# Turning ten more attention blocks of X by DMA, with fewer filling matmuls and a new order of the work

## The chip, the cores and the metric

The kernel runs on one core of one Trainium2 chip. The metric is the device time of one execution in microseconds (us). The program has one queue of instructions for each engine: PE (TensorE, matmuls; PEld is its weight load), DVE (VectorE), ACT (ScalarE), POOL (GpSimd) and SP (SyncE, which here only issues DMAs). Each queue is worked off in its own order; an instruction waits at the head of its queue until what it needs is there, and all behind it wait with it.

## The reference

A gated linear attention is followed by a two-layer network with a leaky ReLU. Shapes: q, k, v and f_logit are (4, 8, 768, 48), that is batch, heads, time, channel; w_in is 384 x 2048 and w_out 2048 x 384; the output is 3072 x 384. All tensors are float32.

```python
f = 1.0 / (1.0 + np.exp(-f_logit))
for t in range(S):
    state = f[:, :, t, :, None] * state + np.einsum('bhd,bhe->bhde', k[:, :, t], v[:, :, t])
    y[:, :, t] = np.einsum('bhd,bhde->bhe', q[:, :, t], state)
x = y.transpose(0, 2, 1, 3).reshape(B * S, H * D)
h = x @ w_in
out = np.maximum(0.01 * h, h) @ w_out
```

## The kernel before, in words

**Units.** Time is cut into 6 chunks of 128 steps, and a unit is one chunk of one batch element: 24 units. Units 0 to 3 are the first chunks of the four batch elements, 4 to 19 the middle chunks, 20 to 23 the last. A unit gives 128 rows of y, called X where it enters the network. Two units make a pair m; pair m holds units 2m and 2m + 1, and its network part works on 256 rows.

**Attention of a unit** from 4 on: three loads (load_part, L168) bring k, q and v; gate_pe (L338) sums the log gates of a group of four units on PE, decay_em and decay_a (L350, L353) make the decays on ACT; k_scale and q_scale (L356, L360) scale k and q on DVE or POOL into the tile kqh; cast_v (L144 or L146) makes bfloat16 v. turn_dma (L372) turns kqh by a transposing DMA into kqT (units 8 to 23; turn_pe, L369, does it on PE for units 4 to 7). score_pe (L394) forms the scores of both units of a pair, mask (L405) masks them on DVE, mix_pe (L412 and L415) gives y, and state_pe, state_dve and state_pool (L423, L431, L432, L437, L296) carry the state on. Units 0 to 3 have functions of their own whose names begin with q_: q_gate_pe L220, q_decay_act L224, casts q_k_cast and q_q_cast (L144 or L146), q_turn_pe L236, products q_k_mul and q_q_mul on DVE (L240), q_score_pe L254, masks q_mask on DVE (L265) and q_mask_pool on POOL (L261), q_mix_pe L271.

**X to the network.** y_out copies a unit's y from PSUM to the bfloat16 tile xn (on ACT or DVE). Then X is turned so that its 384 channels lie on partitions, in one of two ways. x_pe (L446) makes three transposes on PE into PSUM, and x_out copies them to xT on ACT or DVE. x_dma (L376) is one transposing DMA on SP's queue, from xn straight to xT:

```python
def x_dma(u):
    nc.sync.dma_start_transpose(out=x_part(u), in_=xns[u % R_XN])
```

Before the change units 0 to 17 take the first way and 18 to 23 the second.

**Network of a pair.** up (L456; up1, L467, for single units) is six matmuls of 256 columns, eight of them for a pair; up_act (L461) is the leaky ReLU on ACT into gT; down (L476) is eight matmuls of 384 columns for one half of a unit, two halves to a unit; put copies the result to SBUF and out_dma (L499) writes it out. The first halves of the up products (g of 0 to 3) use the first half of w_in, the others the second; each half is one DMA of POOL's queue (load_w_in, L180).

**Filling matmuls.** idle_pe(n, bank) (L138) issues n matmuls on a tile of zeros, whose result nobody reads. Before the change there are 41 ahead of the first gate sums and 2 + 2 + 3 among the first scores.

**Order.** The order is written out by hand: a list of some 800 calls, one line each, at the end of the kernel. Each engine's queue holds its instructions in the order of this list. SP's queue takes the loads, the turns and the outputs in one line, and each of its DMAs also waits for the one issued eight before it. Rings of tiles tie things together: 7 raw tiles each of k, q and v, 4 of kqh, kqT, xn and xT, 5 of gT, 8 of the output.

Of the kernel before, what the change touches and what calls it, by code (L numbers as in the profile page):

```python
# [16 lines left out]
def kernel(  # L17
# [485 lines left out]
    q_ln_act(0)  # L503
    q_k_cast(V, 1)
    q_exp_act(1)
    idle_pe(24, 0)
    q_ln_act(1)
    q_q_cast(G, 1)
    idle_pe(17, 1)
    q_gate_pe(0, 1, 2)  # L510
    q_gate_pe(0, 0, 3)
    load_part(2, 'v', v)
    q_gate_pe(1, 1, 4)
    q_decay_act(0, 0, emT, 1.0, 3)
    q_gate_pe(1, 0, 5)
    q_decay_act(0, 1, emT, 1.0, 2)
    load_part(1, 'v', v)
    q_turn_pe(khq, 1, 1, 6)
    q_decay_act(1, 1, emT, 1.0, 4)
    q_k_cast(A, 0)  # L520
    q_turn_pe(khq, 0, 0, 7)
    q_k_mul(1, 1, 6)
    q_k_mul(0, 0, 7)
    q_turn_pe(khq, 0, 1, 0)
    q_decay_act(1, 0, emT, 1.0, 5)
    q_turn_pe(khq, 1, 0, 1)
    load_part(0, 'v', v)
    q_q_cast(A, 0)
    q_turn_pe(qhq, 1, 0, 6)
    q_decay_act(0, 0, aT, -1.0, 3)  # L530
    load_w_in(0)
    load_w_in(1)
    q_k_mul(0, 1, 0)
    q_decay_act(1, 0, aT, -1.0, 5)
    load_part(3, 'v', v)
    q_turn_pe(qhq, 0, 0, 7)
    load_f(1, 0)
    q_k_mul(1, 0, 1)
    q_q_mul(1, 0, 6)
    load_part(5, 'v', v)  # L540
    q_turn_pe(qhq, 1, 1, 3)
    idle_pe(2, 0)
    q_score_pe(1, 0, 5, 1)
    q_q_mul(0, 0, 7)
    q_decay_act(1, 1, aT, -1.0, 4)
    q_decay_act(0, 1, aT, -1.0, 2)
    q_turn_pe(qhq, 0, 1, 4)
    q_q_mul(1, 1, 3)
    q_q_mul(0, 1, 4)
    load_f(1, 1)  # L550
    cast_v(G, 2)
    load_part(4, 'k', k)
    load_part(4, 'q', q)
    put_rows()
    q_score_pe(0, 0, 2, 6)
    cast_v(A, 0)
    q_back_pe(1, 0)
    q_back_pe(3, 7)
    load_w_out(0)
    q_mask(0, 0, 0, 2)  # L560
    q_score_pe(1, 1, 3, 4)
    q_mask(1, 0, 0, 5)
    q_mask(1, 0, 1, 1)
    q_wf_act(0, 0, 1, 6)
    cast_v(A, 1)
    q_back_out(A, 3, 7)
    q_back_out(A, 1, 0)
    q_mask_pool(0, 0, 1)
    q_back_pe(0, 6)
    q_back_out(A, 0, 6)  # L570
    idle_pe(2, 2)
    q_score_pe(0, 1, 7, 2)
    idle_pe(3, 5)
    q_mix_pe(1, 0)
    q_mask(1, 1, 0, 3)
    q_mask(0, 1, 0, 7)
    q_mask(1, 1, 1, 4)
    upto_pe(1)
    q_mix_pe(0, 5)
    load_part(5, 'q', q)  # L580
    state_pe(1, 6)
    q_wf_act(0, 1, 1, 2)
    state_pe(0, 2)
    y_out(A, 1, 0)
    y_out(A, 0, 5)
    q_back_pe(2, 3)
    cast_v(G, 3)
    q_mask_pool(0, 1, 1)
    x_pe(1, 0)
    q_state_dve(1)  # L590
    x_pe(0, 7)
    load_part(5, 'k', k)
    load_w_out(1)
    q_mix_pe(3, 5)
    x_out(A, 1, 0)
    x_out(A, 0, 7)
    load_part(4, 'v', v)
    state_pe(3, 4)
    y_out(A, 3, 5)
    q_mix_pe(2, 0)  # L600
    load_part(7, 'k', k)
    up(0, 3, 7)
    y_out(V, 2, 0)
    put_upto(V, 1)
    x_pe(3, 6)
    x_out(A, 3, 6)
    x_pe(2, 5)
    up(0, 0, 0)
    q_back_out(A, 2, 3)
    up(0, 1, 1)  # L610
    load_part(6, 'k', k)
    load_part(6, 'q', q)
    x_out(V, 2, 5)
    up(0, 2, 6)
    up(1, 0, 5)
    up_act(0, 1, 1)
    q_state_dve(0)
    up(1, 2, 3)
    up_act(0, 0, 0)
    up(1, 3, 2)  # L620
    up_act(1, 0, 5)
    q_state_pool(0)
    up_act(1, 2, 3)
    up(1, 7, 1)
    gate_exp(1, 0)
    up_act(1, 3, 2)
    up(0, 6, 0)
    up_act(1, 7, 1)
    up_act(0, 3, 7)
    up(0, 7, 5)  # L630
    up(1, 5, 3)
    up(1, 1, 2)
    up(1, 6, 1)
    up(0, 4, 7)
    up_act(0, 7, 5)
    up_act(0, 6, 0)
    up_act(1, 1, 2)
    up(1, 4, 5)
    up_act(0, 2, 6)
    gate_ln(1, 0)  # L640
    up_act(0, 4, 7)
    cast_v(G, 5)
    up(0, 5, 0)
    down(1, 0, 2)
    load_w_out(2)
    up_act(1, 6, 1)
    down(0, 0, 6)
    gate_exp(1, 1)
    load_f(2, 0)
    up_act(0, 5, 0)  # L650
    q_state_dve(3)
    gate_ln(1, 1)
    up_act(1, 4, 5)
    gate_pe(1, 4, 7, 1, 0)
    up_act(1, 5, 3)
    down(2, 0, 5)
    decay_em(6, 1)
    decay_em(4, 4)
    decay_a(4, 4)
    end_pe(1, 3)  # L660
    decay_em(5, 7)
    down(3, 0, 4)
    load_w_out(3)
    decay_em(7, 0)
    load_part(7, 'q', q)
    k_scale(V, 4)
    load_part(7, 'v', v)
    load_part(6, 'v', v)
    decay_a(5, 7)
    q_scale(V, 4)  # L670
    load_f(2, 1)
    cast_v(G, 4)
    turn_pe(4, 7)
    end_act(1, 3)
    turn_k(A, 4, 7)
    state_pe(2, 3)
    decay_a(7, 0)
    down(1, 1, 2)
    k_scale(G, 5)
    turn_q(A, 4, 7)  # L680
    down(2, 1, 5)
    score1_pe(4, 0, 7)
# [12 lines left out]
    mix_pe(4, 1)
    y_out(A, 4, 1)
    load_part(8, 'q', q)
    down(3, 1, 4)
    x_pe(4, 7)
    q_scale(V, 6)  # L700
    state_dve(4)
    load_part(8, 'v', v)
    x_out(V, 4, 7)
    turn_pe(6, 0)
    gate_exp(2, 0)
    turn_k(A, 6, 0)
    load_part(11, 'q', q)
    put(V, 2, 5)
    put(V, 3, 4)
    turn_pe(5, 1)  # L710
    q_scale(G, 7)
    up1(4, 0, 3)
    state_pool(4)
    turn_q(V, 6, 0)
    up1(4, 1, 7)
    up1(4, 2, 5)
    turn_q(A, 5, 1)
    load_part(9, 'v', v)
    turn_pe(7, 4)
    put(V, 0, 6)  # L720
    state_dve(5)
    turn_k(V, 7, 4)
    turn_k(A, 5, 1)
    up_act1(4, 0, 3)
    state_pool(5)
    up1(4, 3, 0)
    turn_q(V, 7, 4)
    score1_pe(5, 1, 6)
    mask(5, 1, 6)
    up_act1(4, 1, 7)  # L730
    up_act1(4, 2, 5)
    mask(5, 0, 1)
    score_pe(3, 3, 7, 2, 5)
    mask(6, 0, 3)
    cast_v(A, 6)
    down(4, 0, 4)
    state_pe(6, 6)
    cast_v(A, 7)
    mix_pe(5, 1)
    mask(6, 1, 7)  # L740
    state_dve(6)
    state_pool(6)
    gate_ln(2, 0)
    gate_exp(2, 1)
    up_act1(4, 3, 0)
    y_out(A, 5, 1)
    down(4, 1, 4)
    x_pe(5, 0)
    load_part(11, 'v', v)
    gate_ln(2, 1)  # L750
    mask(7, 1, 5)
    mask(7, 0, 2)
    x_out(V, 5, 0)
    gate_exp(3, 0)
# [580 lines left out]
```

## Time and profile before

| | us |
|---|---|
| median of 3 runs | 183.28 (182.80, 183.28, 183.33) |
| the profiled execution | 182.37 |
| its span, from first to last instruction | 180.6 |
| PE busy | 173.3 |
| ACT busy | 115.7 |
| DVE busy | 82.7 |
| POOL busy | 57.9 |

The profiled execution took 1.8 us more than its span; these lie before the first and behind the last instruction. In the profile a row of the timeline gives start, length, engine, line of the kernel, operation, tiles (output <- input) and, in brackets, how long the engine had stood idle ahead of it and what ended that. Rows of the critical chain give start, length and what the chain ran through in that stretch.

### The profile page before, as it was taken

The numbers are of one execution on the slowest core, as the hardware profiler recorded it, in microseconds if no ns is written. First come the engines' busy times: TensorE is split into PE (matmuls) and PEld (weight loads), VectorE is DVE, ScalarE is ACT, GpSimd is POOL, SyncE is SP. The second block draws the span as 40 slices with busy tenths as digits, with TensorE's granted clock in tenths as the row PEclk, the third lists the DMA queues.
The fourth block names the chain that finished last, engine by engine and source line by source line (L and its number), as shares of the span: only waits on it lengthen the run. The fifth ranks groups of instructions, "written<-read, shape, count | busy, mean of one in ns | idle before, by whom it ended". The sixth has DMA issues, their size and how long they took to land.

```text
span 180.6 us, 4883 instructions
## 1 busy us (share of the span) xinstructions
PE 173.3 (96%) x1963; PEld 139.7 (77%) x1963; DVE 82.7 (46%) x179; ACT 115.7 (64%) x229; POOL 57.9 (32%) x117
## 2 busy tenths in 40 slices
PE   6999899999999999999999996999999999999992
PEld 4888699766878986699866794887886988788672
DVE  6549850028886454583152565193734780000110
ACT  2777869973789994868787646689362336439101
POOL 8019610306524304596360563325030610000000
PEclk9999999999999999999999999999999999999998
DMA  4899999999998999997999999899986954120132
GB/s 115 243 258 220 189 204 250 172 216 215 208 215 170 213 182 194 221 221 152 280 195 167 194 223 180 165 220 199 207 162 134 164 172 158 22 87 4 40 140 82
DMA packets 99589, 31.83 MB, mean 176 GB/s; under 512 B 86896, under 2 KB 98288, under 8 KB 99568
## 3 DMA queue, kind: packets, MB, share of 16 engines
q1 hardware_dynamic: 97616, 27.99, 78.1%
q0 software_dynamic: 1376, 3.15, 9.2%
q10 hardware_dynamic: 576, 0.39, 0.8%
q8 instruction: 15, 0.25, 0.6%
q14 instruction: 6, 0.05, 0.1%
HBM read 25.17 MB, written 4.72 MB: 166 GB/s over the span
## 4 chain that ended last, share of the span: by engine, by line
PE 78%; DMA 11%; SPq 2%; POOL 2%; issue 2%; ACT 2%; POOLq 0%
PE ps L476 31%; PE ps L456 29%; DMA w_in<-in_moe_w_in_dram 5%; PE ps L467 3%; DMA k_raw<-in_k_dram 2%; SPq L69 2%; PE ps L394 2%; DMA qq<-in_q_dram 2%; PE ps L415 2%; PE ps L338 2%; PE ps L412 2%; DMA fq<-in_f_logit_dram 2%; PE ps L481 1%; PE ps L423 1%; PE ps L446 1%
## 5 line engine op out<-in xcount | busy, mean ns | idle before, releaser
L476 PE MATMUL ps<-w_out_b,gT 128*128 128x384 bf16 x368 | 65.1, 326 | 0.0
L456 PE MATMUL ps<-xT,w_in 128*128 128x256 bf16 x528 | 63.0, 273 | 0.4 <-DMA w_in<-in_moe_w_in_dram 0.4
L461 ACT ACTIVATE gT<-ps 128x512 bf16<-128x512 f32 x88 | 48.7, 611 | 22.8 <-PE ps L456 22.6
L456 PEld LDWEIGHTS <-w_in 128*128 128x128 bf16 x528 | 56.3, 114 | 1.8 <-DMA w_in<-in_moe_w_in_dram 0.6
L476 PEld LDWEIGHTS <-gT 128*128 128x128 bf16 x368 | 34.4, 98 | 21.2 <-issue 0.6
L405 DVE TENSOR_TENSOR wm<-ps,ut 128x512 bf16<-128x512 f32 x40 | 25.4, 684 | 16.3 <-PE ps L394 15.8
L437 POOL TENSOR_TENSOR sf<-sf,a_end 128x192 f32<-128x192 f32 x16 | 8.8, 549 | 28.1 <-DVE sf L432 25.2
L296 POOL CAST sb<-sf 64x192 bf16<-64x192 f32 x40 | 13.7, 343 | 5.3 <-DVE sf L288 2.8
L146 POOL CAST v_b<-v_raw 128x384 bf16<-128x384 f32 x12 | 6.3, 531 | 28.2 <-DMA v_raw<-in_v_dram 28.0
L356 DVE TENSOR_TENSOR kqh<-k_raw,em_t 128x384 bf16<-128x384 f32 x11 | 6.6, 610 | 16.6 <-ACT em_t L350 14.0
L146 DVE COPY qq<-ps 128x384 f32<-128x384 f32 x5 | 2.7, 554 | 24.0 <-PE ps L476 24.0
L144 ACT CAST xn<-ps 128x384 bf16<-128x384 f32 x15 | 7.1, 487 | 8.5 <-PE ps L415 8.5
L356 POOL TENSOR_TENSOR kqh<-k_raw,em_t 128x384 bf16<-128x384 f32 x9 | 8.3, 931 | 12.5 <-PE ps L476 6.1
L144 ACT COPY qq<-ps 128x384 f32<-128x384 f32 (+1 forms) x8 | 3.5, 448 | 13.3 <-PE ps L476 5.1
L350 ACT ACTIVATE em_t<-ps 128x384 bf16<-128x384 f32 x20 | 9.6, 520 | 1.4 <-PE ps L338 1.4
L360 POOL TENSOR_TENSOR kqh<-q_raw,a_t 128x384 bf16<-128x384 f32 x10 | 9.4, 949 | 3.2 <-DMA q_raw<-in_q_dram 2.3
L353 ACT ACTIVATE a_t<-ps 128x384 bf16<-128x384 f32 x20 | 10.0, 525 | 0.3 <-PE ps L338 0.3
L146 DVE CAST xn<-ps 128x384 bf16<-128x384 f32 x9 | 5.0, 555 | 9.0 <-PE ps L415 8.3
L431 DVE TENSOR_TENSOR sf<-sf,ps 64x192 f32<-64x192 f32 x16 | 5.5, 342 | 7.5 <-PE ps L423 5.6
L138 PE MATMUL ps<-fill 128*128 128x256 bf16 x48 | 7.7, 327 | 0.0
L360 DVE TENSOR_TENSOR kqh<-q_raw,a_t 128x384 bf16<-128x384 f32 x10 | 6.4, 649 | 2.6 <-ACT a_t L353 2.5
L423 PE MATMUL ps<-v_b,kqh 128*128 128x96 bf16 x80 | 6.2, 206 | 1.4 <-POOL kqh L356 1.4
(96 smaller groups left out, 206.7 us busy)
## 6 DMA issues: line engine op xcount, KB each, us to landing
v_raw<-in_v_dram SPq DMA_DIRECT2D x24, 192.0 KB, 4.7
k_raw<-in_k_dram SPq DMA_DIRECT2D x20, 192.0 KB, 4.5
q_raw<-in_q_dram SPq DMA_DIRECT2D x20, 192.0 KB, 4.6
out_dram<-osb SPq DMA_DIRECT2D x12, 192.0 KB, 2.7
out_dram<-qq SPq DMA_DIRECT2D x11, 192.0 KB, 2.1
kq<-in_f_logit_dram SPq DMA_DIRECT2D x4, 384.0 KB, 7.3
w_in<-in_moe_w_in_dram POOLq DMA_DIRECT2D x2, 768.0 KB, 10.6
w_out_b<-in_moe_w_out_dram POOLq DMA_DIRECT2D x4, 384.0 KB, 8.5
```

What stands on the lines that cost most here:

```text
L144: eng.copy(out=out, in_=in_)
L146: eng.tensor_copy(out=out, in_=in_)
L296: nc.gpsimd.tensor_copy(out=state_b[n][r, :, e * D:(e + 1) * D], in_=state_f[b][r])
L350: nc.scalar.activation(em_ts[u % R_EM], bank(bk)[:, 0:H * D], AF.Exp, scale=1.0)
L353: nc.scalar.activation(a_ts[u % R_EM], bank(bk)[:, 0:H * D], AF.Exp, scale=-1.0)
L356: eng.tensor_mul(khs[u % R_KQS][:, :, 0:D], raw[u]["k"], em_ts[u % R_EM])
L360: eng.tensor_mul(qhs[u % R_KQS][:, :, 0:D], r["q"], a_ts[u % R_EM])
L405: nc.vector.tensor_mul(wms[e][u % R_WM], bank(bk).rearrange("p (i n) -> p i n", i=P2), ut[:, None, :].to_broadcast([128, P2, 128]))
L437: nc.gpsimd.tensor_mul(sf, sf, a_ends[u // 4 % 2][:, :, u % 4:u % 4 + 1].to_broadcast([128, P2, D]))
L456: nc.tensor.matmul(bank(bk)[:, i * 256:(i + 1) * 256], w_in_p[ff // 8][:, kk, ff // 4 % 2, :, ff % 4], xTs[m % R_XT][:, kk].rearrange("p a ...
L461: nc.scalar.activation(gTs[m % GBUFS][:, 2 * g:2 * g + 2].rearrange("p f a n -> p (f a n)"), bank(bk), AF.Prelu, alpha=0.01)
L476: nc.tensor.matmul(bank(bk)[:, 0:KD], g_part(u)[:, ff, :], w_out_b[:, ff, :], start=(ff == 0), stop=(ff == NF - 1))
```

## The change

Three things change. The units 8 to 17 get x_dma in place of x_pe and x_out, as units 18 to 23 have it already. idle_pe loses ten matmuls ahead of the first gate sums and the seven among the first scores. The list of calls is written out in a new order, from its first line to its last; all other calls are there as often as before, though some have another engine (a cast on DVE in place of ACT) or another PSUM bank.

```diff
-    idle_pe(24, 0)
...
-    idle_pe(17, 1)
+    idle_pe(24, 0)
+    idle_pe(7, 1)
...
-    idle_pe(2, 0)
...
-    idle_pe(2, 2)
...
-    idle_pe(3, 5)
...
-    x_pe(9, 3)
...
-    x_out(V, 9, 3)
-    x_pe(8, 7)
...
-    x_out(V, 8, 7)
...
+    x_dma(8)
...
+    x_dma(9)
```

PE's queue gets 47 matmuls (and as many weight loads) fewer: 30 transposes of X and 17 filling ones. SP's queue gets ten DMAs more.

**DVE at the start.** Here are DVE's rows behind its first clearing of tiles: khq and qhq are the bfloat16 k and q of units 0 to 3 (119 and 121 are heads 0 to 3, 120 and 122 heads 4 to 7), kTq and qTq the products, wm the masked scores. Before:

```order
L146 CAST khq_120<-kq 128x16x48
L240 TENSOR_TENSOR kTq_241<-ps_67,gT_238 128x512
L240 TENSOR_TENSOR kTq_240<-ps_68,gT_238 128x512
L240 TENSOR_TENSOR kTq_240<-ps_61,gT_238 128x512
L240 TENSOR_TENSOR kTq_241<-ps_62,gT_238 128x512
L240 TENSOR_TENSOR qTq_243<-ps_67,gT_237 128x512
L240 TENSOR_TENSOR qTq_242<-ps_68,gT_237 128x512
```

And now:

```order
L146 CAST khq_119<-kq 128x16x48
L146 CAST khq_120<-kq 128x16x48
L146 CAST qhq_121<-qq 128x16x48
L240 TENSOR_TENSOR kTq_240<-ps_67,gT_238 128x512
L240 TENSOR_TENSOR kTq_241<-ps_66,gT_238 128x512
L240 TENSOR_TENSOR qTq_242<-ps_68,gT_237 128x512
L240 TENSOR_TENSOR qTq_243<-ps_64,gT_237 128x512
L240 TENSOR_TENSOR kTq_241<-ps_62,gT_238 128x512
L265 TENSOR_TENSOR wm_215<-ps_67,ut 128x512
L240 TENSOR_TENSOR kTq_240<-ps_61,gT_238 128x512
L265 TENSOR_TENSOR wm_217<-ps_68,ut 128x512
L265 TENSOR_TENSOR wm_221<-ps_64,ut 128x512
```

Two casts that ACT made before are now DVE's, one of them of q, ahead of the first product; and batch elements 2 and 3 (wm_215, 217, 219, 221) are masked ahead of the products of the other two.

**POOL at the start.** These are POOL's rows from its first cast on, w_in_112 and w_in_113 being the two halves of w_in. Before:

```order
L146 CAST qhq_122<-qq 128x16x48
L180 DMA w_in_112<-in_moe_w_in_dram 128x3x1024
L180 DMA w_in_113<-in_moe_w_in_dram 128x3x1024
L146 CAST v_b_206<-v_raw_181 128x384
L312 COPY kqT_213<-ident 128x512
```

And now:

```order
L146 CAST qhq_122<-qq 128x16x48
L180 DMA w_in_113<-in_moe_w_in_dram 128x3x1024
L261 TENSOR_TENSOR wm_219<-wm_219,ut 128x512
L180 DMA w_in_112<-in_moe_w_in_dram 128x3x1024
L185 DMA w_out_b<-in_moe_w_out_dram 128x1536
```

The second half of w_in now goes first, and the first half is issued behind a mask of POOL, which waits for scores of PE. The first seven up calls of the new list use the second half alone.

**SP where units 16 to 19 are turned.** kqT_210 to 213 are the turned kqh of units 16 to 19, xT_226 the turned X of units 16 and 17. Before (their X was turned on PE):

```order
L372 DMA_TRANSPOSE kqT_211<-kqh_129 128x8x128
L499 DMA out_dram<-qq 128x384
L372 DMA_TRANSPOSE kqT_210<-kqh_128 128x8x128
L372 DMA_TRANSPOSE kqT_213<-kqh_131 128x8x128
L168 DMA k_raw_169<-in_k_dram 128x8x48
L168 DMA v_raw_183<-in_v_dram 128x8x48
```

And now:

```order
L376 DMA_TRANSPOSE xT_226<-xn_222 128x3x128
L168 DMA k_raw_170<-in_k_dram 128x8x48
L376 DMA_TRANSPOSE xT_226<-xn_223 128x3x128
L168 DMA v_raw_183<-in_v_dram 128x8x48
L499 DMA out_dram<-qq 128x384
L372 DMA_TRANSPOSE kqT_212<-kqh_130 128x8x128
L372 DMA_TRANSPOSE kqT_213<-kqh_131 128x8x128
L168 DMA k_raw_165<-in_k_dram 128x8x48
```

The turns of X now stand in SP's queue between loads of units that come later, so those loads are issued behind the y_out of units 16 and 17. Counted over the list, from SP's first turn of kqh to its last load of v, the queue held 36 loads of units, 6 of gates, 16 turns of kqh, 2 turns of X and 10 outputs; now it holds 37, 7, 16, 13 and 11.

More of the change, by code (lines that the diff above doesn't have):

```diff
@@ L1216 @@
[L1216 to L1224 removed]
+    y_out(V, 10, 4)
+    up(4, 0, 4)
+    up_act(4, 3, 0)
+    up(4, 5, 5)
+    end_act(3, 1)
+    load_f(4, 0)
+    load_part(12, 'k', k)
+    up(4, 4, 2)
+    up_act(4, 0, 4)
+    up(4, 7, 0)
+    up_act(4, 1, 6)
+    state_pe(11, 1)
+    up_act(4, 5, 5)
+    load_part(13, 'k', k)
+    x_dma(10)
+    decay_em(12, 7)
```

1479 lines of the change are left out of this document (728 added, 751 removed).

## Prediction

> **What bounds the kernel now.** I read the page first (shares of busy time, the slices), then the chain of waits, then the timelines around its steps, and last the DMA rows.
>
> ```profile
> span 180.6 us, 4883 instructions
> PE 173.3 (96%) x1963; PEld 139.7 (77%) x1963; DVE 82.7 (46%) x179; ACT 115.7 (64%) x229; POOL 57.9 (32%) x117
> DMA  4899999999998999997999999899986954120132
> PE 78%; DMA 11%; SPq 2%; POOL 2%; issue 2%; ACT 2%; POOLq 0%
> ```
>
> PE is busy 96% of the span and carries 78% of the chain, so matmul work taken away can be worth time. But the DMA engines are as full as PE until about slice 30, and this change moves work from the one to the other. The chain shows the stages:
>
> ```profile
> 8.62 4.09 DMA qq<-in_q_dram
> ...
> 12.87 0.77 POOL qhq L146
> 13.64 8.78 DMA w_in<-in_moe_w_in_dram
> ...
> 22.46 0.85 PE ps L456 x6
> ...
> 45.40 0.20 PE ps L415 x8
> 45.60 1.30 PE ps L476 x8
> 46.90 0.17 PE ps L446 x3
> ...
> 62.28 0.66 PE ps L456 x6
> ...
> 64.26 0.17 PE ps L423 x4
> ...
> 177.39 0.32 ACT qq L144
> ```
>
> Until 22.46 the chain runs through q, its cast on POOL and the load of w_in; then PE works almost without a break for 154.93 us, to 177.39. In that stretch the PE rows give the price of a call: up 0.66, half a down 1.30, state_pe 0.17, x_pe 0.17, the eight matmuls of 48 columns in a mix_pe 0.20. One break stands out:
>
> ```profile
> 112.21 0.34 PE L423 MATMUL ps<-v_b,kqh 128*128 128x96 bf16 x4 [1.41 <-POOL kqh L356]
> ```
>
> PE stood 1.41 us ahead of a state_pe whose scaled k was late.
>
> **The change, part by part.** The sum is made against the profiled execution: 182.37 us with a span of 180.6. The three runs have a median of 183.28, 0.91 above it; I add that at the end.
>
> *X by DMA.* Ten x_pe at 0.17 leave PE: **-1.7**. The ten x_out leave ACT and DVE, which do not bound, so they count nothing.
>
> *Work moved past the first up.* The new list has two q_mix_pe more behind its first up than the old one. Each is eight matmuls of 48 columns, 0.20: **+0.4**.
>
> *Filling matmuls.*
>
> ```profile
> 1.68 6.46 PE L138 MATMUL ps<-fill 128*128 128x256 bf16 x41
> 7.65 0.85 ACT L215 ACTIVATE lfc<-fq 128x768 bf16<-128x768 f32 x1
> 7.98 3.66 PE L220 MATMUL ps<-steps,lfc 128*128 128x256 bf16 x32
> 9.96 0.56 DVE L146 CAST khq<-kq 128x768 bf16<-128x768 f32 x1 [2.79 <-DMA kq<-in_k_dram]
> 12.22 2.62 DVE L240 TENSOR_TENSOR kTq<-ps,gT 128x512 bf16<-128x512 f32 x4 [1.70 <-ACT khq L144]
> 16.05 1.81 SPq L305 DMA_DIRECT2D kq<-in_f_logit_dram  x1
> 17.80 1.15 POOL L261 TENSOR_TENSOR wm<-wm,ut 128x512 bf16<-128x512 bf16 x1 [0.22 <-ACT wm L258]
> 22.46 0.85 PE L456 MATMUL ps<-xT,w_in 128*128 128x256 bf16 x6 [0.44 <-DMA w_in<-in_moe_w_in_dram]
> 27.45 0.84 ACT L327 ACTIVATE kq<-kq 128x768 f32<-128x768 f32 x1
> 28.19 2.54 ACT L461 ACTIVATE gT<-ps 128x512 bf16<-128x512 f32 x5
> ...
> L144 ACT CAST xn<-ps 128x384 bf16<-128x384 f32 x15 | 7.1, 487 | 8.5 <-PE ps L415 8.5
> ...
> kq<-in_f_logit_dram SPq DMA_DIRECT2D x1, 384.0 KB, 16.6
> ```
>
> 41 of them (0.158 each) ended at about 8.1, and the gate sums began there. Ten fewer would let PE go at 6.6, but the new list begins with the gates of heads 4 to 7, whose logarithm on ACT (7.65 + 0.85) ends at 8.50. The first sums come half a microsecond later, not earlier, and k (9.96) and q (12.7) are still to come. The seven others filled waits. So **0**, with 0 to +0.5 as bounds; the cover is the loads, which set the start anyway.
>
> *First up.* In the new order DVE has q's cast (0.56 like that of k, from the arrival of q at 12.7), then nine products and masks at 0.66 to 0.68 (2.62 for four), which gives 19.3; behind them two q_mix_pe (0.4), two y_out and two x_out on ACT (four at 0.49) and x_pe (0.2): 21.9, or 22.5 with a little wait at each change of engine. w_in's first transfer is issued behind the same cast on POOL as before and landed at 22.42. Both end together, so the first up stays near 22.5: **0**, bounds 0 and +1.5 (a product's 0.66 twice more in the line, where a bank is waited for).
>
> *Waits of ACT's making between 25 and 60.* ACT has to do 16 up_act (five in 2.54 or a little more), and now both halves of gate_exp and one of gate_ln (0.84 each) lie ahead of six of them. Added up in the order of ACT's queue from the first up on, the up_act that the first down needs ends at 34.2 and the one whose bank the gate sums need at 36.8; PE, with 16 up and one down pair (two at 1.30), gets to them at 34.1 and 36.6. Small waits for banks follow in the turns by PE. I take **+0.6**, bounds 0 and +2.0 (if the second gate load lands as late as before, 16.05 + 16.6 = 32.65, ACT stands there from 31.9 on, 0.75, and the turns by PE behind it wait as much again).
>
> *The stall at 112.* k of unit 16 is now issued ahead of the kqh turn of unit 15, before it came behind it, with four gate loads around. I take the 1.41 as gone: **-1.4**, bounds -1.4 and 0.
>
> *DMA.* The ten turns pass through SP's queue, ahead of loads, and through full engines:
>
> ```profile
> L376 SPq DMA_TRANSPOSE xT<-xn x6: 1179/1183/1205, 135.5 to 154.4; - x6
> ...
> DMA to landing us min/median/max: 2.3/2.4/3.2
> ...
> 155.50:156.50 1.00, 1.00 (x9) 0.67 (x8) 0.00 (x0) 0.34 (x1) 0.00 (x0) 1.00 0.49 98
> ...
> 63.20:138.70 75.50, 74.09 (x862) 58.37 (x860) 36.93 (x78) 51.61 (x106) 29.84 (x55) 1.00 1.07 195
> ```
>
> The last turn of X, issued at 154.4, ran alone: a share of 0.49 over 1 us, so 0.49 us of all 16 engines, while it held SP for 1.18. From the first turn of kqh to the last load of v (138.65) the DMA share is 1.07 at 195 GB/s, so what is added there lengthens the stretch. By the list it holds 11 turns of X more, one load of 192 KB (1.0 us at 195 GB/s), one gate load of 384 KB (2.0) and one output (1.0).
>
> ```profile
> 63.23 3.99 SPq L372 DMA_TRANSPOSE kqT<-kqh  x2
> ...
> 138.65 0.58 SPq L168 DMA_DIRECT2D v_raw<-in_v_dram  x1
> ...
> 142.35 0.35 DVE L146 CAST v_b<-v_raw 128x384 bf16<-128x384 f32 x1
> ...
> 149.02 0.33 PE L412 MATMUL ps<-sb,kqT 128*128 128x96 bf16 x4
> ```
>
> The stretch took 75.4 us. With 0.49 a turn it takes 75.4 + 5.4 + 4.0 = 84.8; with 1.18 a turn (nothing passes while SP is held) 92.4. What can it take before PE waits? Before, v of unit 23 was cast 3.7 us after its issue and used by mix_pe only at 149.02, so there was slack. In the new list mix_pe of unit 23 has 21.7 us of PE work from it to the end (two mix_pe, 16 up, six half downs, two column downs). PE without DMA waits would end at 175.3 by the terms above, and reach that mix_pe at 153.6. Less 3.7, a cast of 0.5 on ACT and 0.1, the last load has to be issued by 149.3, 86.1 us after the first turn. So 84.8 fits by 1.3 us and 92.4 is 6.3 too late. The bounds are 0 and +6.3; 0.49 is the one measured on a turn alone, so I stay near it, and take **+0.8**, half of the 1.41 that one late load has cost already.
>
> Sum: -1.7 + 0.4 - 1.4 + 0.6 + 0.8 = **-1.3**: PE's end at 176.1, the profiled execution at 181.1, the median at 183.28 - 1.3 = **182.0**.
>
> **A rule that speaks against it.** A turn of X took 2.3 to 3.2 us from issue to landing, against 0.17 on PE. The Trainium skill, "VectorE: DVE Perf Modes", section "Rules for kernel authors", says to transpose a 128 x 128 block on TensorE when PSUM will do as the destination, and gives 390 ns against 1309 ns for the DMA; the trace agrees with its direction. By that rule the change costs time; by the sum above it does not, as long as PE has other work meanwhile. Whether it has is counted as a rival.
>
> **Rivals.**
>
> *All of it.* No waits of ACT's or the DMA's making: -1.7 + 0.4 - 1.4 = -2.7, which gives **180.6**. For it: the engines beside PE have idle time. Against: before had a late load with fewer DMAs.
>
> *The DMA stretch is too long (slower).* The place is the last units: SP is held by turns of X until y_out of the pair is there, the loads behind are issued late, and PE waits at score_pe of pair 11 or mix_pe of unit 23. It decides from 86.1 us on. At 1.18 a turn PE waits 6.3 in place of 0.8: 182.0 + 5.5 = **187.5**; halfway (0.84 a turn, 88.6 us) 2.5, so 183.7. For it: DMA at 1.07 and SP issuing nearly without a gap. Against: part of SP's time is back-pressure of the same full engines, which would be counted twice.
>
> *w_in's first half is late (slower).* It is issued behind a POOL mask of 1.15. That mask waits for the first scores (three products on DVE, to 15.4, and 0.4 on PE) and a copy on ACT with two moves ahead of it (to 16.8), so it ends at 18.0, and the load goes out at 18.0 to 18.9.
>
> ```profile
> DMA to landing us min/median/max: 8.8/10.6/12.5
> ```
>
> PE needs it behind seven up (4.6) and 1.0 of small work, at 28.1. With 8.8 it lands by 27.7 and costs nothing; with 12.5, at 31, PE waits 2.9: **184.9**. For: the 12.5 is that of the half issued second. Against: that one stood in line behind the other half, which now has four microseconds of lead.
>
> *X late at each pair (slower).* Between the later mix_pe of a pair and its first up the new list has PE work of 5.9, 5.2, 6.8, 5.0 and 6.0 us for pairs 4 to 8, by the prices above. Needed are y_out 0.56, up to 0.6 for the other turn of the pair, the landing and 0.2. At 3.2 that is 4.6 and fits everywhere. The turns of kqh, which ran in the full stretch, took 3.9 in the median and 5.7 at most; at 5.7 it is 7.1, and PE waits 1.2 + 1.9 + 0.3 + 2.1 + 1.1 = 6.6 us: 182.0 - 0.8 + 6.6 = **187.8**. For it: these turns run in the full stretch too. Against: a turn of kqh is two and a half times as large. It is the way in which the rule of the Trainium skill would come true.
>
> ```profile
> DMA to landing us min/median/max: 3.1/3.9/5.7
> ```
>
> **How the numbers follow.** Forecast, with its own spread of a microsecond: 0.44. All of it: 0.10. DMA stretch too long: 0.29, of which the milder part, near 183.5, is 0.05. w_in late: 0.11. X late at each pair: 0.06. A measurement of this kernel can tell about 0.3%, or 0.55 us, from no change. Faster by more than that (below 182.7): 0.38 of the forecast's 0.44 and the 0.10, so 0.48. Within it: 0.06 + 0.05 = 0.11. Slower: 0.24 + 0.11 + 0.06 = 0.41. The likeliest case by itself is 181.0 to 183.0. The range for 8 in 10 goes from 180.2, somewhat under the full gain, to 186.6, short of the two ends at 187.5 and 187.8, which only a part of their cases reach.
>
> **What would show it.** The first up at 22 to 23 and the gate sums of group 1 near 36.8: the start is right. No idle time of PE ahead of L338 or L476 in 30 to 40. L456 of pairs 4 to 8 with no wait for L376: the rule does not bite. The last load of v issued before 149.3 and PE idle ahead of L394 and L412 near 150 under 1 us: the DMA term is right; if that load comes at 152 or later, the DMA rival holds. A new late load of k, as at 112, somewhere between 65 and 130 would be a stall that I did not place, and one or two of them are enough to turn the sign.

## The result, and the profile after

| | before | after |
|---|---|---|
| median beside each other, us | 183.20 (182.80 to 183.33) | 185.87 (185.69 to 186.32) |
| ratio, 95% interval | 1 | 1.0162 [1.0131, 1.0194] |
| the profiled execution, us | 182.37 | 185.69 |
| its span, us | 180.6 | 183.9 |
| first up, us | 22.46 | 23.25 |
| gate sums of group 1 (L338), us | 36.00 | 37.93 |
| PE's end (last down_cols), us | 177.35 | 180.35 |

The change made the kernel 1.6% slower; 182.0 was forecast. On another chip the ratio was 1.0195 [1.0135, 1.0254] (run e15 below). Ratios leave disturbed runs out, so where a ratio and the medians beside it differ, the ratio is the one to use.

The page of after, in the order span, PE, DMA's slices, chain:

```profile
span 183.9 us, 4774 instructions
PE 171.8 (93%) x1916; PEld 136.6 (74%) x1916; DVE 88.6 (48%) x191; ACT 109.5 (60%) x216; POOL 53.7 (29%) x108
DMA  4899999999988999596999798997798696552213
PE 60%; DMA 24%; SPq 7%; ACT 2%; issue 2%; POOL 2%; DVE 1%; POOLq 0%; DVEq 0%
```

PE is busy 1.5 us less than before and the span is 3.3 us longer. The share of the chain on PE fell from 78% to 60%; DMA and SP's queue together have 31% of it where they had 13%. The last chain thus runs through transfers that before lay beside PE. Note the DMA slices: before, they stood at 8 or 9 in nearly every place up to slice 29; now there are 5, 6 and 7 among them from slice 17 on. So the transfers reach further to the end while the engines are less full.

PE's rows with idle time, from the first up on:

```profile
23.25 0.85 PE L456 MATMUL ps<-xT,w_in 128*128 128x256 bf16 x6 [0.78 <-DMA w_in<-in_moe_w_in_dram]
29.31 6.09 PE L456 MATMUL ps<-xT,w_in 128*128 128x256 bf16 x54 [0.30 <-DMA w_in<-in_moe_w_in_dram]
105.10 0.82 PE L456 MATMUL ps<-xT,w_in 128*128 128x256 bf16 x6 [1.59 <-DMA xT<-xn]
145.81 1.48 PE L456 MATMUL ps<-xT,w_in 128*128 128x256 bf16 x12 [0.29 <-DMA xT<-xn]
155.57 0.40 PE L394 MATMUL ps<-kqT 64*128 64x128 bf16 x8 [0.67 <-DMA kqT<-kqh]
```

The wait of 1.41 for k of unit 16 at 112 is gone. In its place stand waits for w_in (both halves), for the turned X of pair 6, for that of unit 18 and for the last turned kqh. The longest, 1.59 at the first up of pair 6, can be followed back on DVE (the two y_out of units 12 and 13) and on SP's queue:

```profile
96.09 0.56 DVE L146 CAST xn<-ps 128x384 bf16<-128x384 f32 x1 [0.64 <-issue]
...
97.32 0.56 DVE L146 CAST xn<-ps 128x384 bf16<-128x384 f32 x1
```

```profile
92.81 2.71 SPq L372 DMA_TRANSPOSE kqT<-kqh  x1
...
96.86 2.63 SPq L372 DMA_TRANSPOSE kqT<-kqh  x1
...
100.22 2.51 SPq L376 DMA_TRANSPOSE xT<-xn  x2
...
150.28 3.28 SPq L372 DMA_TRANSPOSE kqT<-kqh  x2
...
154.91 0.58 SPq L168 DMA_DIRECT2D v_raw<-in_v_dram  x1
```

The y of unit 12 was in xn at 96.65 and that of unit 13 at 97.88. SP issued their turns between 100.22 and 102.73, behind a turn of kqh that held it for 2.63 us. The last row is the last load of v: 94.1 us after the first turn of kqh (60.83), where 75.4 lay between the two before. Over that time the engines were less full than before (the column ahead of GB/s is the DMA share):

```profile
60.83:154.91 94.08, 91.83 (x1002) 71.38 (x1000) 44.57 (x90) 57.61 (x115) 31.78 (x60) 1.00 0.95 184
```

0.95 at 184 GB/s, where before it was 1.07 at 195. Two things must be known to read this. The count ahead of the prediction is wrong in one number: up to its last load of v the old list has 14 turns of kqh, not 16. The new list has all 16 there, and the rows at 150.28 are those of units 22 and 23. And the late load itself cost PE nothing: its v was cast by 158.50, and PE reached the mix that reads it at 158.69, without a wait.

```profile
157.99 0.51 ACT L144 CAST v_b<-v_raw 128x384 bf16<-128x384 f32 x1 [4.32 <-DMA v_raw<-in_v_dram]
```

```profile
158.69 0.36 PE L415 MATMUL ps<-v_b,wm 128*128 128x48 bf16 x8
```

The other place is the start. POOL's rows:

```profile
13.06 1.21 POOL L146 CAST qhq<-qq 128x768 bf16<-128x768 f32 x1 [7.11 <-DMA qq<-in_q_dram]
14.21 0.94 POOL L180 DMA_DIRECT2D w_in<-in_moe_w_in_dram  x1
18.21 1.15 POOL L261 TENSOR_TENSOR wm<-wm,ut 128x512 bf16<-128x512 bf16 x1 [3.06 <-ACT wm L258]
19.31 0.81 POOL L180 DMA_DIRECT2D w_in<-in_moe_w_in_dram  x1
```

The cast ahead of w_in takes 1.21 us here and took 0.83 before; q itself came 0.19 later. The first half of w_in goes out at 19.31 and PE waits 0.30 for it at 29.31.

PE's end moved by +3.0. In that sum the work behind the first up is -1.3, the first up +0.8, the stall at 112 -1.4, the five waits above without the first one +2.9, two of 0.2 for ACT +0.3, and 1.7 lie in gaps too small for rows of their own.

### The profile page after: what moved, and what is told of

Read it like the earlier page. It is cut to its first block, busy times and chain, and to the rows that moved or that the text cites. A ratio compares the mean times of both kernels' runs of the same rounds, so it can differ in the third digit from the quotient of the medians.

```text
span 183.9 us, 4774 instructions
## 1 busy us (share of the span) xinstructions
PE 171.8 (93%) x1916; PEld 136.6 (74%) x1916; DVE 88.6 (48%) x191; ACT 109.5 (60%) x216; POOL 53.7 (29%) x108
## 4 chain that ended last, share of the span: by engine, by line
PE 60%; DMA 24%; SPq 7%; ACT 2%; issue 2%; POOL 2%; DVE 1%; POOLq 0%; DVEq 0%
PE ps L456 24%; PE ps L476 20%; DMA w_in<-in_moe_w_in_dram 5%; DMA v_raw<-in_v_dram 4%; PE ps L467 3%; DMA out_dram<-osb 3%; DMA q_raw<-in_q_dram 2%; DMA qq<-in_q_dram 2%; SPq L69 2%; SPq L372 2%; DMA xT<-xn 2%; PE ps L338 2%; DMA k_raw<-in_k_dram 2%; DMA kqT<-kqh 2%; DMA fq<-in_f_logit_dram 2%
## 5 line engine op out<-in xcount | busy, mean ns | idle before, releaser
L476 PE MATMUL ps<-w_out_b,gT 128*128 128x384 bf16 x368 | 65.1, 326 | 0.2 <-ACT osb L144 0.2
L476 PEld LDWEIGHTS <-gT 128*128 128x128 bf16 x368 | 34.3, 98 | 21.9 <-issue 1.4
L296 POOL CAST sb<-sf 64x192 bf16<-64x192 f32 x40 | 15.0, 374 | 7.4 <-DVE sf L288 5.1
L356 DVE TENSOR_TENSOR kqh<-k_raw,em_t 128x384 bf16<-128x384 f32 x14 | 8.6, 617 | 7.5 <-DMA k_raw<-in_k_dram 7.3
L146 DVE COPY qq<-ps 128x384 f32<-128x384 f32 x8 | 4.4, 556 | 15.9 <-PE ps L476 14.2
L360 DVE TENSOR_TENSOR kqh<-q_raw,a_t 128x384 bf16<-128x384 f32 x11 | 6.0, 556 | 11.3 <-ACT a_t L353 10.2
L356 POOL TENSOR_TENSOR kqh<-k_raw,em_t 128x384 bf16<-128x384 f32 x6 | 5.8, 973 | 17.5 <-ACT gT L461 8.7
L144 ACT CAST xn<-ps 128x384 bf16<-128x384 f32 x11 | 5.1, 486 | 9.4 <-PE ps L415 7.6
L146 POOL CAST v_b<-v_raw 128x384 bf16<-128x384 f32 x7 | 3.5, 505 | 23.4 <-DMA v_raw<-in_v_dram 23.3
L144 ACT CAST v_b<-v_raw 128x384 bf16<-128x384 f32 x12 | 6.2, 519 | 5.8 <-DMA v_raw<-in_v_dram 5.8
L146 DVE CAST xn<-ps 128x384 bf16<-128x384 f32 x13 | 7.0, 554 | 4.8 <-PE ps L415 4.0
L415 PE MATMUL ps<-v_b,wm 128*128 128x48 bf16 x160 | 7.4, 183 | 0.0
L224 ACT ACTIVATE gT<-ps 128x512 f32<-128x512 f32 x8 | 4.3, 611 | 5.1 <-PE ps L220 5.1
```

The source lines that it names most:

```text
L144: eng.copy(out=out, in_=in_)
L146: eng.tensor_copy(out=out, in_=in_)
L296: nc.gpsimd.tensor_copy(out=state_b[n][r, :, e * D:(e + 1) * D], in_=state_f[b][r])
L356: eng.tensor_mul(khs[u % R_KQS][:, :, 0:D], raw[u]["k"], em_ts[u % R_EM])
L360: eng.tensor_mul(qhs[u % R_KQS][:, :, 0:D], r["q"], a_ts[u % R_EM])
L476: nc.tensor.matmul(bank(bk)[:, 0:KD], g_part(u)[:, ff, :], w_out_b[:, ff, :], start=(ff == 0), stop=(ff == NF - 1))
```

## The experiments

Three theories were tried. **Queue theory**: X by DMA lays ten turns into SP's line, and what hangs on that line comes late. **Order theory**: the new list costs the time, however X is turned, its start above all. **Fillers**: the filling matmuls were worth something.

### Parts alone

**e1: X by DMA in the old order.**

```diff
-    x_pe(9, 3)
+    x_dma(9)
...
-    x_out(V, 9, 3)
...
```

(the same for units 8 to 17)

> The order of before, with X of units 8 to 17 turned by DMA at the places where PE turned it, nothing else changed. Queue theory (the ten turns of X hold SP's queue for about 2.5 us each, and what is loaded behind them comes late): the 1.7 us that PE saves is overtaken by waits of PE for late turns and loads, 184.5 to 187. Order theory (the loss comes from the new order of the work, its start above all, and X by DMA is a gain by itself): 181.3 to 182.2.

The median is 198.18 us beside 183.50, the ratio 1.0645 [1.0576, 1.0715]; the profiled execution took 196.15 us. PE's waits for xT by the view of waits (total, times, longest), one of them, and what stood ahead of the turn on SP and ACT:

```profile
PE ps L456 <- DMA xT<-xn: 7.9, 3, 4.0
```

```profile
88.05 3.45 PE L456 MATMUL ps<-xT,w_in 128*128 128x256 bf16 x18 [3.98 <-DMA xT<-xn]
```

```profile
81.72 0.48 ACT L144 CAST xn<-ps 128x384 bf16<-128x384 f32 x1 [0.75 <-PE ps L415]
```

```profile
83.47 1.60 SPq L168 DMA_DIRECT2D v_raw<-in_v_dram  x1
85.17 1.20 SPq L376 DMA_TRANSPOSE xT<-xn  x1
```

The y of unit 10 was ready at 82.20 and its turn issued at 85.17, behind the turn of unit 11, an output and a load of v; PE went on at 88.05. That is 5.9 us from y to up, where x_pe (0.17) and a copy on DVE (0.36) were all that lay between. The old order leaves no such time between a pair's y and its first up. The loss is more than three times what the queue theory allowed: X itself came late, not only the loads behind it. A part of it is not waits but clock: the granted clock was 0.74 from 85 to 90 us, 0.92 to 95, 0.86 from 135 to 140 and 0.80 to 145, which is some 3.4 us by an estimate from these figures.

**e2: the new order, X on PE.**

```diff
+    x_pe(16, 6)
+    x_out(A, 16, 6)
...
-    x_dma(16)
...
```

(units 8 to 17, each in a bank that was free at that place; y_out of unit 17 on DVE)

> The order of after, with X of units 8 to 17 turned on PE again (x_pe and x_out put where a bank is free). Queue theory: PE has 1.7 us more to do, but the waits for X of pair 6 (1.6 us), for X of unit 18 (0.3) and for the last turns (0.7) go, and the start stays 0.8 late: 184.5 to 185.2. Order theory: the waits stay or come back in another place, and the 1.7 us are added to 185.9: 187.0 to 187.8.

186.54 us beside 183.50; ratio 1.0157 [1.0111, 1.0203], against 1.0162 for after. Neither bound was met. The waits for X are gone, but x_pe now waits at three places (0.5, 0.4 and 0.3 us), and the wait for w_in was 1.4:

```profile
PE ps L456 <- DMA w_in<-in_moe_w_in_dram: 1.4, 1, 1.4
...
PE ps L446 <- DVE xn L146: 0.5, 1, 0.5
PE ps L446 <- ACT qq L144: 0.4, 1, 0.4
PE ps L446 <- ACT a_t L353: 0.3, 1, 0.3
```

So in the new order X by DMA neither gains nor loses that can be measured. The 1.2 us of waits at x_pe belong to the places that I chose, and the first up came at 24.15, 0.9 later than in the profiled execution of after.

The run shows one thing more. From the first turn of kqh to the last load of v, SP's line took as long here, without the ten turns of X in it, as in after (94.08):

```profile
62.02:155.31 93.29, 92.00 (x1020) 72.61 (x1019) 47.47 (x100) 57.05 (x115) 30.32 (x60) 1.00 0.89 175
```

So it is the new order that makes this stretch long and the share low, not the ten turns; and with the last load this late PE waits for no transfer behind its first up.

**e3: fewer fillers in the old order.**

```diff
-    idle_pe(17, 1)
+    idle_pe(7, 1)
```

> The order of before with 7 filling matmuls in place of 17 ahead of the first gate sums, nothing else changed. If the fillers only fill a wait of PE: 183.0 to 183.4, with the first gate sums at the same time as before and a granted clock of 0.99 or more. Rival (they keep TensorE's clock up for the start): a lower clock in the first 40 us and 183.8 to 185.

183.46 beside 183.50; ratio 1.0021 [0.9990, 1.0052], clock 0.998. The ten fillers ahead of the gate sums cost nothing that can be told from no change, as forecast. The seven among the first scores were not tried by themselves.

**e4: of after, only X of units 12 and 13 on PE.**

```diff
-    x_dma(12)
...
-    x_dma(13)
...
+    x_pe(12, 2)
+    x_out(V, 12, 2)
...
+    x_pe(13, 6)
+    x_out(V, 13, 6)
```

> Of after, only X of units 12 and 13 turned on PE again. Queue theory: the wait of 1.6 us at the first up of pair 6 goes and 0.34 us of PE's work comes: 184.4 to 184.8. Rival (the time gained there is only waited for later, at a load or an output): 185.6 to 186.2.

The median is 186.07 (183.31 to 189.68), the ratio 1.0045 [1.0002, 1.0088]. The wait of pair 6 went, and from the gate sums of group 1 to PE's end the profiled execution took 139.8 us (40.58 to 180.39), 2.6 less than after. But its start was worse:

```profile
24.80 0.85 PE L456 MATMUL ps<-xT,w_in 128*128 128x256 bf16 x6 [2.01 <-DMA w_in<-in_moe_w_in_dram]
```

```profile
25.00:40.00 15.00, 15.00 (x136) 13.36 (x135) 2.85 (x8) 11.54 (x21) 2.35 (x5) 0.89 1.01 186
```

After the wait of 2.01 the granted clock was 0.89 over 15 us, another 1.6. So the place is mended, as the queue theory says. How much of the whole time that is worth is not settled with a spread of 6 us: the ratio gives about 184.3 us, close to the queue theory, and the median lies in the rival's range.

### The start

**e6: both halves of w_in issued together.**

```diff
     load_w_in(1)
+    load_w_in(0)
...
-    load_w_in(0)
```

> Of after, only the issue of w_in's first half moved up behind that of the second half. Start theory: the first half lands before 27, the wait of 0.3 us for it goes, the first up stays at 23.3: 185.4 to 185.8. Rival (shared DMA engines): the second half lands later than 23.2, and the first up moves to 24 or later: 186.2 to 187.

186.75 (184.27 to 188.90), ratio 1.0133 [1.0070, 1.0197]. That interval holds the 1.0162 of after: nothing gained that can be told. Between the theories it does not decide: the median lies in the rival's range, and in the profiled execution the first up came at 24.50, as the rival has it, but the ratio by itself gives about 185.5 us, as the start theory has it.

**e5: w_in ahead of the cast.**

```diff
-    q_q_cast(G, 1)
+    q_q_cast(V, 1)
...
+    touch('q')
     load_w_in(1)
+    load_w_in(0)
...
-    load_w_in(0)
```

> Of after, only the loads of w_in: the second half of q is cast by DVE in place of POOL, POOL touches one element of q and issues the second half of w_in at once, and the first half right behind it. Start theory (1.9 us of the loss at the gate sums of group 1 come from POOL's cast of 1.21 us ahead of the first w_in issue, and from the late issue of the other half): the first w_in issue about 0.2 us after q lands in place of 1.2, the first up 1 us earlier (22.2 to 22.8 with q landing at 12.9), no wait for w_in after it, and 0.8 to 1.6 us off the time of after: 184.3 to 185.1. Rival (the halves share the DMA engines, and what is gained at the issue is lost in the landing): the first up at 23.3 or later and 185.6 to 186.6.

186.82 (185.89 to 188.61), ratio 1.0210 [1.0161, 1.0260]. No gain. In the profiled execution q came only at 14.15, and no wait for w_in was left, but PE waited 2.0 for the cast of q on DVE that after has as well, and the first up came at 25.16. In the other profiled executions that cast began at 12.8 to 13.7, so this one shows a late q more than it shows the edit; the six runs together show no gain.

**e8: e5 and e4 together.** The diff is that of both.

> After with the w_in edit of the start and with X of units 12 and 13 turned on PE: both places together. If these two places hold the whole loss: 185.9 less 1.2 at the start less 1.3 at pair 6, so 183.0 to 183.8, level with before. Rival (there is a third place of the new order that costs 1 us or more): 184.5 to 185.5.

185.80, ratio 1.0160 [1.0114, 1.0205]: above even the rival's bound. Here q came at 13.03, w_in was issued at 13.57 and the first up ran at 23.00, so the start was mended, and the gate sums of group 2 came at 54.53, where e4 had them at 57.97. Yet PE ended 2.2 us later than in e4 (182.62 against 180.39):

```profile
73.70 0.83 PE L338 MATMUL ps<-lfc,upto 32*128 32x384 bf16 x16 [0.88 <-ACT lfc L330]
...
87.80 5.40 PE L456 MATMUL ps<-xT,w_in 128*128 128x256 bf16 x48 [1.46 <-DMA xT<-xn]
101.13 0.83 PE L338 MATMUL ps<-lfc,upto 32*128 32x384 bf16 x16 [0.90 <-ACT lfc L330]
```

Two calls of SP's queue in both, first e8, then e4:

```profile
67.60 1.23 SPq L372 DMA_TRANSPOSE kqT<-kqh  x1
...
74.42 4.39 SPq L376 DMA_TRANSPOSE xT<-xn  x2
```

```profile
66.66 2.16 SPq L372 DMA_TRANSPOSE kqT<-kqh  x1
...
74.92 3.77 SPq L376 DMA_TRANSPOSE xT<-xn  x2
```

PE was 3.4 us ahead, and SP's queue stood where it stands with a late PE: one call 0.9 later, the other 0.5 earlier. What PE had won it waited for at the gates and at X. This turned the question from the start to the pace of the transfers.

### The one stall that the change removed

**e7: k of unit 16 earlier, in the old order.**

```diff
+    load_part(16, 'k', k)
     load_part(17, 'q', q)
...
-    load_part(16, 'k', k)
```

> The order of before, with only the load of k of unit 16 moved up on SP's queue, ahead of the load of q of unit 17. If the wait of 1.4 us of PE for k of unit 16 is the one term that the new order gains: it goes, nothing else comes late, and 1.2 to 1.4 us go off the time of before: 181.9 to 182.3. Rival (PE then waits for what was moved behind it, q of unit 17, or for the gate of the last group): 182.8 to 183.5.

182.85 beside 183.10; ratio 0.9983 [0.9959, 1.0008]: not told from no change, the rival. POOL and PE:

```profile
110.53 0.99 POOL L360 TENSOR_TENSOR kqh<-q_raw,a_t 128x384 bf16<-128x384 f32 x1 [2.81 <-DMA q_raw<-in_q_dram]
111.49 0.90 POOL L356 TENSOR_TENSOR kqh<-k_raw,em_t 128x384 bf16<-128x384 f32 x1
```

```profile
112.44 0.35 PE L423 MATMUL ps<-v_b,kqh 128*128 128x96 bf16 x4 [1.00 <-POOL kqh L356]
```

POOL stood at the product of q of unit 17, now the late one, with that of k of unit 16 queued behind it. So the load that was moved up could do little while its consumer stood behind one that waited.

**e17: the consumer too.**

```diff
+    k_scale(G, 16)
     q_scale(G, 19)
...
-    k_scale(G, 16)
```

(with the edit of e7)

> Before with k of unit 16 loaded ahead of q of unit 17, as in the earlier run, and POOL's product for k of unit 16 moved up too, ahead of those for q of units 19 and 17. In the earlier run POOL waited 2.8 us for q of unit 17 with the product for k of unit 16 queued behind it. If that was what kept 1.0 us of the wait: the wait at 112 goes whole, and 1.2 to 1.4 us off before: 181.8 to 182.3. Rival (the next late thing is q of unit 17 itself, or the turn of unit 17): 182.6 to 183.4.

182.79 beside 183.20; ratio 0.9965 [0.9931, 0.9998]. The wait at 112 is gone; one of 0.35 for the turn of pair 8 at 115.73 is left. The median lies in the rival's range: the wait went as expected, but not 1.2 us with it. The whole gain is 0.02 to 0.7%. Of the kernels that leave nothing out it is the only one faster than both, and barely.

### The two orders joined

**e9 to e12**: the list of the one kernel up to and with the gate sums of group 1, and from there what is left of the other's, in the other's order, with banks given out anew where they clashed. e9 has the start of before and the rest of after; e10 the reverse; e11 is e9 with X of units 12 and 13 on PE; e12 is e9 with X of units 8 to 17 on PE.

```diff
     gate_pe(1, 4, 7, 1, 0)
+    state_pe(2, 5)
+    load_part(7, 'q', q)
+    up_act(1, 5, 3)
...
```

> The order of before up to and with the gate sums of group 1, and from there the order of after (X by DMA in it). Start theory: the gate sums of group 1 come at 36.0 to 36.6 in place of 37.9 in after, the rest runs as in after (142.4 us from there to PE's end), and the time is 184.0 to 184.6. Rival (SP's queue of loads and turns sets the pace of the rest, so that an earlier PE only waits longer in it, as in the run with both places mended): 185.4 to 186.4, with new waits of PE for X, k and q or gates.

> The other half: the order of after up to and with the gate sums of group 1, and from there the order of before (X of units 8 to 17 on PE). Start theory: 1.9 us later at the gate sums, the rest as in before (141.4 us): 184.8 to 185.5. Rival (the loss lies in the rest of the new order): 183.0 to 183.8.

> The start of before, the rest of after with X of units 12 and 13 on PE. Start theory, with the wait of pair 6 as the second place: 139.8 us from the gate sums of group 1 (36.0 to 36.6) to PE's end, and 181.3 to 182.5, which is below before. Rival (SP's queue sets the pace of the rest): 183.5 to 185.5.

> The start of before, the rest of after with X of all ten units 8 to 17 on PE. If X by DMA saves PE's 1.7 us in this order: 1.3 to 1.9 us slower than the same kernel with X by DMA. If what it saves is given back in waits (queue theory): the two within 0.5 us of each other. If X by DMA costs more than it saves: this one is 0.5 us or more faster.

Ratios 1.0442 [1.0409, 1.0475], 1.0329 [1.0303, 1.0354], 1.0340 [1.0296, 1.0384] and 1.0540 [1.0501, 1.0578]. The first three lie outside every bound and are no evidence on either theory; e12 has a bound relative to e9 (below). The seam itself stalls. In e10 PE waits for the last load of w_out_b, which stood on POOL behind a cast that waited 9.76 us for v:

```profile
46.37 3.77 PE L476 MATMUL ps<-w_out_b,gT 128*128 128x384 bf16 x12 [3.03 <-DMA w_out_b<-in_moe_w_out_dram]
```

Between 40 and 60 us all four lost some 4 to 6 us to PE's waits and a lower clock, by an estimate from their rows. In e9:

```profile
46.00:60.00 14.00, 12.90 (x169) 9.73 (x168) 11.15 (x25) 7.31 (x13) 6.01 (x13) 0.88 1.09 207
```

What can be taken from them is e12 against e9 (the same seam): 1.0540 against 1.0442, and 192.94 against 191.31 us. So with X on PE this list is 1% slower, 1.6 us, which is the case in which X by DMA saves PE's 1.7 us. After and e2 were level. Behind the stall at the seam the transfers may have had time to spare; that was not tried further.

### The pace of the transfers

**e13 and e14: half of the late loads.** In after and in before, v from unit 7 on and k and q from unit 11 on are loaded for heads 0 to 3 only. These kernels leave out a part of the input; their instructions are the same.

```diff
-        nc.sync.dma_start(out=t, in_=src[b, :, c * C:(c + 1) * C, :].rearrange("h t d -> t h d"))
+        n = H if u < (7 if name == "v" else 11) else H // 2
+        nc.sync.dma_start(out=t[:, 0:n], in_=src[b, 0:n, c * C:(c + 1) * C, :].rearrange("h t d -> t h d"))
```

> After with half of each late load: v from unit 7 on and q and k from unit 11 on are loaded for heads 0 to 3 only (the other heads keep an earlier unit's data, so part of the input is not read); every instruction elsewhere stays. Pace theory (in the new order PE waits because SP's queue and the DMA engines run full from 45 to 155 us): the waits of PE for X, turned q and k and gates after 60 us go, 2 to 3 us in all: 182.8 to 184.2. Rival (the waits are latencies of the new order, place by place, and its start): the waits stay where they are, 185.2 to 186.2.

> Before with the same halves of the late loads left out. It has one wait that hangs on a load, that for k of unit 16 (1.4 us): 181.6 to 182.4 by both theories. If it gains 2 us or more, DMA takes more of the time of before than its waits show.

**e15: after once more, beside them.**

> After unchanged, on this chip beside the others, for its median and its spread over more runs: 185.5 to 186.4 if the first four runs stand for it. If the new order is one whose time hangs on when the loads land, the runs spread over 3 us or more, as those of its variants did; before spread over 1 us there.

| beside before at 183.20 | median, us | ratio, 95% interval |
|---|---|---|
| after (e15) | 187.55 (184.95 to 188.92) | 1.0195 [1.0135, 1.0254] |
| after, half loads (e13) | 182.04 (181.35 to 183.60) | 0.9947 [0.9917, 0.9978] |
| before, half loads (e14) | 181.49 (181.00 to 181.93) | 0.9907 [0.9872, 0.9942] |

All of PE's waits in e13, then its stretch from the first turn on, and the last load of v:

```profile
PE ps L221 <- ACT lfc L216: 2.0, 1, 2.0
PE ps L119 <- POOL rep L87: 1.6, 1, 1.6
PE ps L457 <- DMA w_in<-in_moe_w_in_dram: 1.2, 1, 1.2
PE ps L237 <- DVE qhq L146: 0.9, 1, 0.9
```

```profile
60.90:150.00 89.10, 89.10 (x989) 70.69 (x987) 44.98 (x90) 56.59 (x115) 31.18 (x60) 1.00 0.80 148
```

```profile
149.90 0.58 SPq L169 DMA_DIRECT2D v_raw<-in_v_dram  x1
```

(Lines behind 168 are one higher here.) From the first up on PE has no wait left, and it is busy for all of the 89.10 us. With nothing moved and the same instructions on the engines, lighter loads give after 2.5% (5.5 us by the medians), more than the pace theory asked, and before 0.9% (1.7 us, of which its one wait on a load is 1.41). Without the pressure of the loads the two differ by 0.4%, with intervals that overlap. So what after loses against before hangs on when transfers land. After itself, in e15, was slower than the 186.4 expected at most, and its spread of 4 us is the one expected of a time that hangs on them.

The profiled executions of e15 and e13 show where. They run in step up to 100 us: first up at 23.80 and 23.77, gate sums of group 1 at 38.29 and 38.27, of group 2 at 55.64 and 55.67. PE ends at 182.22 and 176.44. All of the 5.8 us come behind 100 us: e15 waits 1.26 and 0.44 there for turned X, 0.66 for a mask and 1.45 for the last turned kqh, and 2.0 lie in gaps too small for rows.

The stretch of e13, in which PE never waits, is still 89 us long. That much of PE's work lies between the first turn of kqh and the last load of v in the new list.

**e18: X on PE and half loads.** The diffs of e2 and e13 together.

> The order of after with X of units 8 to 17 on PE, and the same halves of the late loads left out. With the loads light, PE's work alone should count: if the ten turns by DMA save what the prediction said, this is 1.4 to 2.0 us above the run of after with half loads (182.0), so 183.4 to 184.0; the same kernel with full loads took 186.5, so the turns' part in the waits of after would be about as large as the 1.7 us that they save. Rival (X by DMA saves nothing even with light loads, since x_pe fits beside other waits): 181.8 to 182.6.

185.60 beside 183.03; ratio 1.0151 [1.0110, 1.0193], above both bounds. Light loads, which gave after 2.5%, gave this one nothing that can be told (1.0157 with full loads). These two ran on different chips, each beside its own before. With X on PE the new order does not hang on the loads in a way that shows; with X by DMA it does. With light loads X by DMA is 2% better than X on PE, and with full loads the two are level: what the turns save on PE is lost to waits on transfers. The 2% are more than the 1.7 us forecast; x_pe waits 1.3 us in e18 at the places I chose, and the profiled execution, the slowest of the six, started later (first up at 24.99, 23.77 in e13), so this does not price the ten turns cleanly.

**e19: outputs off SP's queue.**

```diff
-        nc.sync.dma_start(out=out[...], in_=st[u].pop("osb"))
+        nc.scalar.dma_start(out=out[...], in_=st[u].pop("osb"))
```

> After with the 23 whole outputs issued from ACT's queue in place of SP's; the bytes and their order stay. If it is SP's queue that paces (each issue and each wait in it holds the loads and turns behind it), its 23 issues of 0.4 to 2.2 us leave it: 183.8 to 185.4. If it is the 16 DMA engines, the same bytes cross them: 186.5 to 188.5, like after on a chip beside. A slower result than that would be ACT itself, held by outputs ahead of its evictions.

189.08 (186.17 to 191.67), ratio 1.0198 [1.0144, 1.0251]. Freeing SP of 23 issues gained nothing, and X of pair 6 was even later:

```profile
107.61 0.82 PE L456 MATMUL ps<-xT,w_in 128*128 128x256 bf16 x6 [2.23 <-DMA xT<-xn]
...
120.01 3.44 PE L456 MATMUL ps<-xT,w_in 128*128 128x256 bf16 x30 [1.34 <-ACT osb L144]
```

The second row is ACT, held as feared, so the run does not say cleanly what the outputs' place in SP's line costs: the median fits an ACT that is held, and the ratio (about 186.7 us) fits the 16 engines. What holds X back, the 16 engines or SP held by the turns themselves, stays open. The share of 0.95 over the stretch does not decide it either, since e2 had 0.89 there and no wait for a transfer. Turns issued from a queue of their own were not tried.

## Why the prediction was wrong, point by point

**The step that failed is the DMA term**, put at +0.8 with bounds 0 and +6.3. It asked one question, whether the last load of v comes in time for the last mix_pe, and priced the ten turns by the length of the stretch up to that load: 84.8 us needed, 86.1 allowed. The stretch took 94.1, the load was issued at 154.91 in place of 149.3 at the latest, and PE did not wait for it. Nor do the ten turns make the stretch long: it took 93.3 without them (e2), and 89.1 with half loads and PE never waiting (e13). The count that it was added to was short as well, by two turns of kqh (14 in the old list, not 16).

What the term left out are the waits on transfers along the way: in after 1.59 for X of pair 6, 0.29 for that of unit 18 and 0.67 for the last turned kqh, and small gaps behind 100 us. In place of 0.8 us the pressure of the loads cost after 4.5 us by the ratios of e13 and e15 (5.5 by the medians). Which part of the transfers' path makes them late is open (e19).

The rival of a DMA stretch that is too long named 183.7 to 187.5, which holds the 185.87, and a last load at 152 or later. That it came out is in part luck: at its place, the last scores and mixes, PE lost 0.67, and its sign shows in e2 too, where nothing waits for a transfer behind the first up.

*X by DMA, -1.7, and work past the first up, +0.4.* Right. With light loads PE took 152.67 us from the first up to its end (23.77 to 176.44); the forecast without its two waits is 176.1 - 0.6 - 0.8 - 22.5 = 152.2. The two terms are shown by their sum, not one by one.

*Fillers, 0.* Right for ten of the 17 (e3).

*First up, 0 with bounds 0 and +1.5.* Too low: +0.8, and 0.3 at 29.31. I took POOL's cast at its old price (0.83) though a cast of DVE now runs beside it; it took 1.21. The landing of w_in moves with q from run to run: across the profiles the first up comes 9.4 to 10.4 us after q with the old start, 10.2 to 11.5 with that of after.

*ACT's waits, +0.6.* Too high, if anything. PE has no wait ahead of L338 or L476 in 30 to 40. From the first up to the gate sums of group 1 it took 14.68 us in place of 13.54; of the 1.14 more, 0.57 are the two q_mix_pe and a state_pe that now stand there and 0.30 the wait for w_in, so at most 0.3 is left.

*The stall at 112, -1.4.* Right, it is gone. It could be removed in the old order as well (e17), so it is no merit of the new one; there it was worth 0.7% at most.

*w_in's first half late.* It landed at 29.27 and cost 0.30, not 2.9.

*X late at each pair.* One pair of five (1.59), and unit 18 (0.29). In the old order, which has no such PE work between y_out and up, it came true (e1: three waits, 7.9 us in all). The rule of the Trainium skill, "VectorE: DVE Perf Modes", section "Rules for kernel authors", to transpose on TensorE when PSUM will do, is borne out by e1 (1.0645). After and e2 are level (1.0162 and 1.0157), and with light loads it does not hold (0.9947 in e13 with X by DMA, 1.0151 in e18 with X on PE).

## What to carry to other kernels

A transfer moved into a busy queue is not priced by asking whether the queue's last load still comes in time: here that load came as late without the ten turns, and cost nothing. Price each place where an engine needs what the queue brings, with the issue and landing times seen under full loads. If an order lives near its transfers' pace, an earlier PE only waits longer: thin the loads once, with everything else unchanged, to see how much of the time hangs on them before mending single waits. And a load that is moved up needs its consumer moved past whatever waits ahead of it.

## What the runs showed of the hardware

*Two casts at once.* POOL's cast of 128x768 from float32 took 0.83 us in before, e3 and e7, and 1.21 in after, e2 and e4, where DVE makes a cast of the same kind from 13.03 to 13.59 beside it in after. That the second causes the first was not tried by itself.

*The clock after a short wait.* Behind waits of 1.88, 1.96 and 2.01 us at the first up (e18, e6, e4) the granted clock was 0.89 over the next 15 us; behind waits of 1.33 to 1.43 there (e2, e14, e15) it stayed at 1.00. The length of the wait alone does not decide it: the wait of 2.23 at 107.61 in e19 was not followed by a lower clock. The Trainium skill, "TensorE: Matmul & The Clock Gate", section "Part 1: The HAM clock gate", has a free-running window of about 3.4 us that must be idle; these waits are shorter, so that rule alone does not give them. Whether short gaps around them count was not tried.

*The issue of a turn.* A turn of kqh held SP for 1.23 us at the least and 1.43 in the median in after, up to 3.01; with half loads 1.27 in the median and 1.89 at most. By the DMA share of the stretch the medians are 1.27 at 0.80 (e13), 1.24 at 0.89 (e2), 1.43 at 0.95 (after) and 1.43 at 1.07 (before).
